# Attention over 128 queries a step, from queries, keys and values that the host lays out, with the softmax sums from a column of ones

## The chip, the cores and the metric

The kernel runs on one NeuronCore of a Trainium2 chip (trn2), as one program. The number that counts is the device time of one execution in microseconds (us). The core has five engines that run beside each other, each in its own instruction order: TensorE (PE in the rows: matrix products and the weight loads, PEld, that go with them), VectorE (DVE), ScalarE (ACT), GpSimd (POOL) and SyncE (SP, which here issues nearly all transfers). 16 DMA engines move data between the chip's memory (HBM) and the on-chip SBUF. Products land in PSUM, which has eight banks of 512 32-bit numbers in each of 128 partitions.

## The reference, cut to what matters

Three layers follow each other: a windowed attention, a mixture of 8 experts in which each token goes to at most one, and a dense layer of two matrices. The change is in the attention and in how the attention is joined to the routing of the experts.

```python
# q, k, v: [2, 8, 768, 64]  (batch, heads, sequence, head size), float32
k_sum = k.reshape(B, H, nb, 32, D).max(axis=3)          # 24 blocks of 32 keys
v_sum = v.reshape(B, H, nb, 32, D).mean(axis=3)
scores_l = scale * q @ k.T     # kept where |query - key| < 16, -1e9 elsewhere
scores_s = scale * q @ k_sum.T + np.log(32)
a = softmax(concat(scores_l, scores_s))                 # sum + 1e-9 below
x = a @ concat(v, v_sum)       # -> [1536 tokens, 512]
# routing: do_compute = x @ w_skip > 0 ; expert = argmax(x @ w_gate) ; gate = its softmax
x[do_compute] += gate * (relu(x @ w1[e]) @ w2[e])
h = x @ w_in ; out = (max(h,0) + alpha * min(h,0)) @ w_out   # w_in, w_out given as float64
```

## The kernel before, in words

`tile_kernel` has four stages. **Attention** works on 64 queries of all 8 heads at a time, in 24 sub-steps (`subs`, 12 for each batch entry). For a sub-step, 96 keys around the queries and the 24 block keys make 120 columns (`NK`). `sub_s` puts the mask into one PSUM bank with a 16-bit product, and adds four products over it, one for each pair of heads: the two heads of a pair stand in the 128 rows of the array, and `qbd` holds their queries block-diagonally, so half of each weight tile is zeros. DVE takes the row maxima, ACT the exponentials with their sums (`accum_out`), POOL divides by the sums (`sub_n`). `sub_t` turns the result by four PE transposes, ACT copies it, and `sub_x` multiplies it with the values, eight products with 64 weight columns each (L327). Two sub-steps fill 128 tokens, which go out to HBM (`xd`) and are turned once more (`tile_xt`); `tile_lt` and `tile_lg` compute their routing logits, in two products with a copy between.

Queries, keys and values arrive as the reference holds them. So keys and queries are copied into another order (`stage`), turned on PE (`first_k`, `prep_k`, `prep_q`), and copied into windows or into `qbd`; the values come as 256-byte pieces (`load_vwin`).

The order of all engines in this stage is the order of the code (`manual_schedule`): a loop over the sub-steps in which the parts of several sub-steps are interleaved, with lists `todo[n]` for what else belongs to sub-step n (loads, preparation, and the 12 weight pieces of 1 MB each that are loaded ahead). `late` and `after` put copies off to a later place. SP issues transfers in that order too; an issue that waits holds back all behind it. The rows of DMA issues wait for the one eight places before.

**Routing** turns logits into lists: `route_a` (best expert), `route_b` (ranks, on PE), `route_l` (places and gates), `route_c` (one-hot rows), `route_d` (the lists, on PE). It runs for four groups of token tiles, the last two after the last sub-step. `route_end` writes the lists (`lidx`), and eight products that nobody reads follow (`warm`, L542). **Experts** gather the rows of `xd` by the lists and work through 8 experts; their weights come through a ring of buffers whose pieces are released as experts finish. **The dense layer** closes the kernel. The last two stages aren't touched by the change.

Of the kernel before, what the change touches and what calls it, by code (L numbers as in the profile page):

```python
# [22 lines left out]

def bf16_parts(x, n):
    out = []
    for _ in range(n):
        b = (np.float32(x).view(np.uint32) + np.uint32(0x8000)) & np.uint32(0xFFFF0000)
        h = float(b.view(np.float32))
        out.append(h)
        x = x - h  # L30
    return out


@with_exitstack
def tile_kernel(ctx: ExitStack, tc: tile.TileContext, q, k, v, w_skip, w_gate, w1, w2, w_in, w_out, alpha, out):
    nc = tc.nc
    B, H, S, D = q.shape
    NP = H // 2
    NS = S // 64
    NB = S // 32  # L40
    NC = S // 256
    NK = 120
    LT = 3
    LX = 4
    NV = 4
    RB = 4
# [28 lines left out]
    qbd = []  # L75
    for i in range(2):
        qbd.append(apool.tile([128, 4, NP, 2, 64], F32, name=f"qbd{i}"))

    def clear(t, eng):
        eng.memset(t[0:64, :, :, 1, :], 0.0)  # L80
        eng.memset(t[64:128, :, :, 0, :], 0.0)

    clear(qbd[0], nc.vector)


    sel = apool.tile([67, 128], BF16, name="sel")
    nc.gpsimd.memset(sel, 1.0)
    nc.gpsimd.memset(sel[0:64, :], 0.0)
    nc.gpsimd.affine_select(
        out=sel[0:64, :].rearrange("p (h x) -> p h x", h=2), in_=sel[0:64, :].rearrange("p (h x) -> p h x", h=2),  # L90
        pattern=[[0, 2], [-1, 64]], compare_op=ALU.not_equal, fill=1.0, base=0, channel_multiplier=1,
    )
    mask = apool.tile([67, 3, NK], BF16, name="mask")
    nc.gpsimd.memset(mask, 0.0)
    logs = bf16_parts(math.log(32.0), 3)
    mlog = mask[64:67, :, 96:NK]
    nc.gpsimd.memset(mlog, logs[0])
    for i in (1, 2):
        nc.gpsimd.affine_select(
            out=mlog, in_=mlog, pattern=[[0, 3], [0, NK - 96]], compare_op=ALU.not_equal, fill=logs[i],  # L100
            base=-i, channel_multiplier=1,
        )
    for a, off in enumerate((0, 16, 32)):
        m = mask[0:64, a, 0:96]
        nc.gpsimd.affine_select(
            out=m, in_=m, pattern=[[-1, 96]], compare_op=ALU.is_gt, fill=-1.0e9,
            base=off + 16, channel_multiplier=1,
        )
        nc.gpsimd.affine_select(
            out=m, in_=m, pattern=[[1, 96]], compare_op=ALU.is_gt, fill=-1.0e9,  # L110
            base=16 - off, channel_multiplier=-1,
        )

    wg = const.tile([128, KC, 32], F32, name="wg")
    nc.gpsimd.memset(wg, 0.0)
    clear(qbd[1], nc.gpsimd)

    avg = apool.tile([128, 16 + NB], F32, tag="lt", bufs=2, name="avg")
    nc.gpsimd.memset(avg, 1.0 / 32.0)
    nc.gpsimd.affine_select(  # L120
        out=avg, in_=avg, pattern=[[-16, 16 + NB]], compare_op=ALU.is_ge, fill=0.0, base=256, channel_multiplier=1)
    nc.gpsimd.affine_select(
        out=avg, in_=avg, pattern=[[16, 16 + NB]], compare_op=ALU.is_ge, fill=0.0, base=15 - 256, channel_multiplier=-1)

    def win(s):
        return (0, 0) if s == 0 else ((2, 32) if s == NS - 1 else (1, 16))

# [56 lines left out]
    def first_k(c):  # L184
# [19 lines left out]
        if c == 1:  # L204
            for g in range(NP):
                for r in range(2):
                    part(kb[g], 64, 0, 1)
# [1096 lines left out]
```

## Time and profile before

| | us |
|---|---|
| median of 3 runs (lowest, highest) | 544.69 (544.65, 547.13) |
| the profiled execution | 544.38 |
| its span, first to last instruction | 542.6 |
| attention, to the end of the last logits product | about 104.3 |
| rest of the attention and the routing, to the lists | 104.3 to 123.3 |
| experts, and the change-over to the dense layer | 127.5 to about 300 |

Busy shares of the whole span are PE 92%, DVE 58%, POOL 36%, ACT 30%, but a stage has its own limit, and the stages follow each other. A row of the timeline merges instructions of one line: its start, its length and the count of records. A float32 product has two records (an 8-product line shows x16), a transpose or a 16-bit product one. As products are pipelined, the cost of a line is read from its start to the start of the next, and not from its length, which has the latency of the last product in it.

### The profile page before, as it was taken

To read this page: it belongs to the slowest core of one execution; us is meant where nothing else is said; L and a number is where in the kernel's file an instruction comes from. 1 tells how busy PE (TensorE), PEld (TensorE's weight loads), DVE (VectorE), ACT (ScalarE), POOL (GpSimd) and SP (SyncE) were. 2 spreads that over 40 slices of the span, in tenths; PEclk is the share of its full clock that TensorE was granted. 3 is DMA by queue.
4 is the path that set the end of the run, shared out by engine and by line. 5 is a ranking of instruction groups with operands and counts; after the bars stand their busy time and mean duration, and the time that the engine had idled before them with its cause. 6 is when DMAs were issued, how large, how long until landed. Compare 5 with 4: busy or idle time off the path is not lost.

```text
span 542.6 us, 8283 instructions
## 1 busy us (share of the span) xinstructions
PE 498.7 (92%) x2999; PEld 372.7 (69%) x2999; DVE 313.4 (58%) x632; ACT 164.9 (30%) x452; POOL 193.9 (36%) x196
## 2 busy tenths in 40 slices
PE   7988999978899999596499899999999999999997
PEld 5577888853454454265277788888888888888885
DVE  4579666476431854289999739893624324243333
ACT  3666677730011110333444442531120101101010
POOL 5285523336220310324853244733453221212121
PEclk9989999998999999898879999999999999999999
DMA  9899979863999583484445402210000000001022
GB/s 240 229 257 247 278 208 277 240 212 109 383 390 396 183 296 118 150 267 143 136 156 170 142 0 79 77 39 1 0 1 0 2 0 2 0 1 59 20 77 77
DMA packets 66820, 76.81 MB, mean 142 GB/s; under 512 B 23358, under 2 KB 46930, under 8 KB 66764
## 3 DMA queue, kind: packets, MB, share of 16 engines
q1 hardware_dynamic: 55916, 59.67, 35.4%
q10 hardware_dynamic: 9408, 14.68, 8.5%
q0 software_dynamic: 1440, 1.76, 1.0%
q8 instruction: 29, 0.48, 0.4%
q14 instruction: 27, 0.22, 0.1%
HBM read 71.00 MB, written 7.91 MB: 145 GB/s over the span
## 4 chain that ended last, share of the span: by engine, by line
PE 49%; DVE 4%; POOL 2%; issue 1%; DMA 1%; ACT 1%; ACTq 0%; POOLq 0%; DVEq 0%
PE o L1242 24%; PE g L1219 24%; POOL wl L1183 1%; DMA raw<-in_moe_w_in_dram 1%; PE ph L945 1%; DVE f L643 1%; DVE f L649 1%; DVE f L648 1%; DVE xl L1081 1%; DVE acc L1252 1%; PE x2p L1204 0%; DVE f L641 0%; POOL glo L1227 0%; ACT raw L644 0%; ACT acc L1250 0%
## 5 line engine op out<-in xcount | busy, mean ns | idle before, releaser
L1227 POOL TENSOR_TENSOR glo<-gs,ghi 128x512 fp32r<-128x512 f32 x48 | 66.7, 1390 | 157.1 <-ACT ghi L1225 157.1
L1222 DVE TENSOR_SCALAR gs<-g,al 128x512 f32<-128x512 f32 x48 | 35.9, 749 | 109.7 <-PE g L1219 109.7
L1225 ACT CAST ghi<-gs 128x512 fp32r<-128x512 f32 x48 | 29.9, 622 | 176.4 <-PE o L1242 150.9
L1242 PE MATMUL o<-woh,ghi 128*128 128x512 f32 x192 | 76.3, 397 | 5.3 <-ACT ghi L1225 5.3
L1242 PE MATMUL o<-woh,glo 128*128 128x512 f32 x192 | 76.4, 398 | 3.0 <-POOL glo L1227 3.0
L1242 PE MATMUL o<-wl,ghi 128*128 128x512 f32 x192 | 76.4, 398 | 0.0
L1219 PE MATMUL g<-xh,wih 128*128 128x512 f32 (+1 forms) x196 | 53.6, 395 | 2.7 <-DVE xl L1081 1.4
L1219 PE MATMUL g<-xl,wih 128*128 128x512 f32 (+1 forms) x196 | 53.0, 390 | 1.1 <-DVE xl L1081 1.1
L1219 PE MATMUL g<-xh,wl 128*128 128x512 f32 (+1 forms) x196 | 51.5, 385 | 0.0
L1242 PEld LDWEIGHTS o<-woh,ghi 128*128 128x128 f32 x192 | 36.4, 190 | 13.7 <-ACT ghi L1225 5.5
L1219 PEld LDWEIGHTS g<-xh,wih 128*128 128x128 f32 x196 | 36.8, 190 | 11.4 <-issue 1.7
L1242 PEld LDWEIGHTS o<-woh,glo 128*128 128x128 f32 x192 | 36.3, 189 | 11.9 <-POOL glo L1227 3.8
L1219 PEld LDWEIGHTS g<-xl,wih 128*128 128x128 f32 x196 | 36.6, 188 | 9.5 <-DVE xl L1081 1.5
L1242 PEld LDWEIGHTS o<-wl,ghi 128*128 128x128 f32 x192 | 36.5, 190 | 8.2
L1219 PEld LDWEIGHTS g<-xh,wl 128*128 128x128 f32 x196 | 36.4, 188 | 7.8
L945 PE MATMUL ph<-w,gTa 128*64 128x512 f32 x128 | 32.9, 626 | 9.4 <-PEq L1148 5.5
L305 POOL TENSOR_TENSOR p<-p,sm 128x480 f32<-128x480 f32 x23 | 24.1, 1049 | 47.2 <-DVE sm L304 21.5
L293 ACT ACTIVATE p<-s,nm 128x120 f32<-128x120 f32 x96 | 33.5, 365 | 22.7 <-DVE sm L303 19.7
L644 ACT ACTIVATE raw<-raw 128x512 f32<-128x512 f32 x32 | 21.7, 684 | 42.6 <-DVE f L643 41.0
L1223 DVE SCALAR_TENSOR_TENSOR gs<-g,gs 128x512 f32<-128x512 f32 x48 | 33.0, 687 | 1.0
L1183 POOL TENSOR_TENSOR wl<-f,wih 128x512 fp32r<-128x512 f32 x16 | 23.3, 1462 | 20.7 <-ACT wih L1182 18.7
L648 DVE SCALAR_TENSOR_TENSOR f<-raw,f 128x512 int32<-128x512 int32 x32 | 30.4, 954 | 0.3
(213 smaller groups left out, 816.4 us busy)
## 6 DMA issues: line engine op xcount, KB each, us to landing
w<-in_moe_w_dram SPq DMA_DIRECT2D x30, 1024.0 KB
raw<-in_moe_w_in_dram ACTq DMA_DIRECT2D x14, 512.0 KB
raw<-in_moe_w_out_dram ACTq DMA_DIRECT2D x14, 512.0 KB
vt<-in_v_dram SPq DMA_DIRECT2D x24, 192.0 KB
rawqst<-in_q_dram SPq DMA_DIRECT2D x6, 512.0 KB
rawkst<-in_k_dram SPq DMA_DIRECT2D x6, 512.0 KB
xd<-x SPq DMA_DIRECT2D x12, 256.0 KB
out_dram<-acc SPq DMA_DIRECT2D x12, 256.0 KB
```

The costliest lines, as they stand in the source:

```text
L293: nc.scalar.activation(p[:, g, :], sp[:, g, :], AF.Exp, bias=nm[:, g:g + 1], scale=1.0, accum_out=sm[:, g:g + 1])
L305: eng.tensor_tensor(out=p, in0=p, in1=sm.to_broadcast([128, NP, NK]), op=ALU.mult)
L644: nc.scalar.activation(raw.bitcast(F32)[:, :, 0], raw.bitcast(F32)[:, :, 1], AF.Abs)
L648: nc.vector.scalar_tensor_tensor(out=f, in0=m1, scalar=-0x40000000, in1=f, op0=ALU.bitwise_and, op1=ALU.bitwise_or)
L945: nc.tensor.matmul(hp[e][64 * h:64 * h + 64, :], gT[g][:, kc, o:o + 64], a[kc // 2][:, kc % 2, 512 * h:512 * h + 512], start=(kc == 0), st ...
L1183: nc.gpsimd.tensor_tensor(out=lo, in0=f, in1=hi.bitcast(F32), op=ALU.subtract)
L1219: nc.tensor.matmul(ph[:, o], a[:, kc, :], x[kc // 2][:, kc % 2, o], start=(i == 0), stop=(i == 3 * KC - 1))
L1222: nc.vector.tensor_scalar(out=g, in0=ph, scalar1=0.0, scalar2=al[:, j:j + 1], op0=ALU.min, op1=ALU.mult)
L1223: nc.vector.scalar_tensor_tensor(out=g, in0=ph, scalar=0.0, in1=g, op0=ALU.max, op1=ALU.add)
L1225: nc.scalar.copy(ghi, g)
L1227: nc.gpsimd.tensor_tensor(out=glo, in0=g, in1=ghi.bitcast(F32), op=ALU.subtract)
L1242: nc.tensor.matmul(po[i], a[:, o], x, start=(jj == 0 and p == 0), stop=(jj == JC - 1 and p == 2))
```

## The change

The host now lays out its inputs (`layouts`), and only the new layouts are passed: `qt` (queries with the head size in the rows, two heads above each other), `kwin` (for each sub-step of 64 queries the 96 keys, turned, and 24 empty columns), `vwin` (for two sub-steps the 96 value rows, with a 1 behind each head's 64 values), `vtok` and `vblk` (values for the block sums), `wgs` and `als`. The transposes, copies and rearrangements of queries and keys go. `block_k` takes the block maxima from the loaded windows and copies them into the empty columns.

A step has 128 queries, and there are 12. `sub_s` issues four mask products and 16 logits products, each with 64 rows and 64 weight columns: head of the pair r chooses the rows and the PSUM bank, half of the queries c chooses the columns. The exponentials have no `accum_out`: the sum comes out of the value product as its 65th column (block rows hold 32 there, and block sums of values in place of means), and `sub_n` divides the product, on DVE, instead of the probabilities, on POOL. The routing logits are one product over 9 columns for each 128 of the 512 features, in `tile_lg`. `late` and `after`, the weave of the last routing groups and `warm` go; PSUM has three banks for logits, and one (`ps_m`) for all of transposed tokens, routing logits, ranks and lists, where three stood.

```diff
-    ps_s = att.enter_context(tc.tile_pool(name="ps_s", bufs=2, space=PSUM))
+    ps_s = att.enter_context(tc.tile_pool(name="ps_s", bufs=3, space=PSUM))
-    ps_m = att.enter_context(tc.tile_pool(name="ps_m", bufs=3, space=PSUM))
+    ps_m = att.enter_context(tc.tile_pool(name="ps_m", bufs=1, space=PSUM))
...
+    def load_k(b, g):
+        kw[b, g] = (kpool, apool)[b].tile([128, NS, NK], F32, tag=f"kw{g}", name=f"kw{b}_{g}")
+        nc.sync.dma_start(kw[b, g], kwin[b, g])
+    def block_k(b, g, spread):
+        m = apool.tile([128, NB], F32, tag="km", bufs=2, name=f"km{b}_{g}")
+        nc.vector.tensor_reduce(
+            out=m.rearrange("p (s n) -> p s n", s=NS),
+            in_=kw[b, g][:, :, 16:80].rearrange("p s (n i) -> p s n i", n=2), axis=AX.X, op=ALU.max)
+        spread(out=kw[b, g][:, :, NWK:NK], in_=m[:, None, :].to_broadcast([128, NS, NB]))
...
-        nc.tensor.matmul(sp, sel, mask[:, win(s)[0], None, :].to_broadcast([67, NP, NK]), start=True, stop=False)
-        for g in range(NP):
-            nc.tensor.matmul(
-                sp[:, g, :], d[:, s % 4, g].rearrange("p h x -> p (h x)"), kw[b, g][:, s, :], start=False, stop=(g == NP - 1))
+        for c in range(2):
+            for r in range(2):
+                s = 2 * t + c
+                w = 0 if s == 0 else (2 if s == NS - 1 else 1)
+                nc.tensor.matmul(
+                    sp[r][64 * c:64 * c + 64], sel[64 * r:64 * r + 64, :],
+                    mask[64 * r:64 * r + 64, w, None, :].to_broadcast([64, NP, NK]), start=True, stop=False)
+        for g in range(NP):
+            for c in range(2):
+                for r in range(2):
+                    o = 128 * (t % 2) + 64 * c
+                    nc.tensor.matmul(
+                        sp[r][64 * c:64 * c + 64, g, :], qs[64 * r:64 * r + 64, g, o:o + 64],
+                        kw[b, g][64 * r:64 * r + 64, 2 * t + c, :], start=False, stop=(g == NP - 1))
...
-            nc.scalar.activation(p[:, g, :], sp[:, g, :], AF.Exp, bias=nm[:, g:g + 1], scale=1.0, accum_out=sm[:, g:g + 1])
+            nc.scalar.activation(
+                p[:, g, :], st["s", n][r][:, g, :], AF.Exp, bias=st["nm", n][:, r, g:g + 1], scale=1.0)
...
-        eng.tensor_tensor(out=p, in0=p, in1=sm.to_broadcast([128, NP, NK]), op=ALU.mult)
+    def sub_x(n):
+        st["x", n] = xp = ps_x.tile([128, 2, 512], F32, tag="x", name=f"xp{n}")
+        for h in range(H):
+            for c in range(2):
+                nc.tensor.matmul(
+                    xp[64 * c:64 * c + 64, h // 4, DV * (h % 4):DV * (h % 4) + DV],
+                    ts[h % 2][:, h // 2, 64 * c:64 * c + 64], vt[b][:, 2 * (t % 2) + c, h, :], start=True, stop=True)
+    def sub_n(n):
+        x = st.pop(("x", n))[:, :, 0:4 * DV].rearrange("p k (h e) -> p k h e", h=4)
+        nc.vector.tensor_scalar(out=sm, in0=x[:, :, :, D:DV], scalar1=1e-9, scalar2=None, op0=ALU.add)
+        nc.vector.reciprocal(out=sm, in_=sm)
+        nc.vector.tensor_tensor(
+            out=t.rearrange("p (k h d) -> p k h d", k=2, h=4), in0=x[:, :, :, 0:D],
+            in1=sm.to_broadcast([128, 2, 4, D]), op=ALU.mult)
+        nc.sync.dma_start(xd[128 * n:128 * n + 128, :], t)
...
+        for c in range(KC):
+            nc.tensor.matmul(ps, xT[:, c, :], wg[:, c, :], start=(c == 0), stop=(c == KC - 1))
...
+    load_q(0, 0)
+    for g in range(NP):
+        load_k(0, g)
+    for c in range(NCH):
+        load_vtok(c)
...
+    for n in range(TT):
+        sub_s(n)
+        if n >= 3:
+            tile_xt(n - 3)
+        sub_m(n)
+        sub_e(n, 0)
+        if n >= 1:
+            sub_t(n - 1, 0, V)
+            sub_t(n - 1, 1, A)
+        sub_e(n, 1)
+        if n >= 2:
+            sub_x(n - 2)
+            sub_n(n - 2)
+        if n >= 3:
+            tile_lg(n - 3)
+        for f in todo[n]:
+            f()
...
+    n = TT - 1
+    tile_xt(n - 2)
+    sub_t(n, 0, V)
+    sub_t(n, 1, A)
+    sub_x(n - 1)
+    sub_n(n - 1)
+    tile_lg(n - 2)
+    for f in todo[TT]:
+        f()
+    sub_x(n)
+    tile_xt(n - 1)
+    route_a(*G[2])
+    sub_n(n)
+    tile_lg(n - 1)
+    route_b(*G[2])
+    route_l(*G[2], [])
+    tile_xt(n)
+    tile_lg(n)
+    for t in range(*G[2]):
+        route_c(t)
+    route_d([4, 5, 6, 7])
+    route_a(*G[3])
+    route_b(*G[3])
+    route_l(*G[3], range(*G[3]))
+    route_d(list(range(8, TT)))
+    route_end()
-    warm(WARM[2])
```
```

On PE, a sub-step of the kernel before in its steady part stands so (the names: `s` logits, `pt` transposed probabilities, `xp` the value product, `qps` transposed queries, `lt` routing products):

```order
L284 LDWEIGHTS sel
L284 MATMUL s_3_1099<-mask,sel 128x480
L286 MATMUL s_3_1099<-kw_0_520,qbd_87 128x120
L286 MATMUL s_3_1099<-kw_1_585,qbd_87 128x120
L286 MATMUL s_3_1099<-kw_2_646,qbd_87 128x120
L286 MATMUL s_3_1099<-kw_3_766,qbd_87 128x120
L311 MATMUL pt_0_1116<-ident,p_0_949 120x128 x4
L327 MATMUL xp_10_1076<-vt_131,ts_11_1095 64x64 x8
L268 MATMUL qps_2_0_1130<-ident,qst_2_1085 128x128 x4
L432 MATMUL lt_1137<-xT_1097,wg 32x128 x4
```

In the changed kernel the end of the logits of one step of 128 queries, and what follows on PE, stand so (four mask products `L171` and 14 more rows of `L178` stand ahead of it, and six more of `L210` and the four products of `tile_lg` behind it):

```order
L178 MATMUL s_0_1139<-kw_3_502,q_2_877 64x120
L178 MATMUL s_1_1140<-kw_3_502,q_2_877 64x120
L281 MATMUL xtp_1161<-ident,x_1114 128x128 x4
L199 MATMUL pt_0_1176<-ident,p_0_1070 120x128 x4
L199 MATMUL pt_1_1183<-ident,p_1_1089 120x128 x4
L210 MATMUL xp_1195<-vt_111,ts_0_1080 64x65 x2
L210 MATMUL xp_1195<-vt_111,ts_1_1087 64x65 x2
```

A logits product has become four of a quarter the tile, the two value products of 64 queries have become one set that alternates between the halves of the array, and `qps` and `lt` are gone from the row.

On DVE, the last routing before the lists is woven in the kernel before: the one-hot rows (`ohb`) stand between steps of `route_a` and ahead of the copies of logits (`lg`):

```order
L502 TENSOR_TENSOR loc<-r_s_1788,r_s_1706 128x2
L488 CAST val<-r_es_1780 128x2
L514 TENSOR_SCALAR ohb_1794<-rows,loc 128x512
L443 COPY lg<-lg_1771 128x9
L443 COPY lg<-lg_1799 128x9
L452 TENSOR_REDUCE r_mx_1802<-lg 128x2
L454 TENSOR_SCALAR r_act_1804<-lg 128x2
L456 TENSOR_TENSOR r_ex_1806<-lg,r_mx_1802 128x16
L459 TENSOR_TENSOR r_oh_1809<-lg,r_mx_1802 128x16
L461 TENSOR_SCALAR r_s_1811<-r_act_1804 128x2
L462 TENSOR_TENSOR r_oh_1809<-r_oh_1809,wt 128x16
L514 TENSOR_SCALAR ohb_1794<-rows,loc 128x512
```

In the changed kernel, at the same place, the copy of the last logits comes first, and the one-hot rows and the sum of lists (`acc`) stand ahead of the last `route_a`:

```order
L351 TENSOR_TENSOR loc<-r_s_1485,r_s_1446 128x2
L337 CAST val<-r_es_1477 128x2
L290 COPY lg<-lg_1498 128x9
L358 TENSOR_SCALAR ohb_1504<-rows,loc 128x512
L358 TENSOR_SCALAR ohb_1506<-rows,loc 128x512
L375 TENSOR_TENSOR acc<-acc,lps_1508 128x20
L301 TENSOR_REDUCE r_mx_1527<-lg 128x2
L303 TENSOR_SCALAR r_act_1529<-lg 128x2
L305 TENSOR_TENSOR r_ex_1531<-lg,r_mx_1527 128x16
```

So DVE has the same instructions there, but waits for PE (`lg`, `acc`) before work that is ready.

## Rows read from the trace of the kernel before

**Rows 1.** Windows: length, busy us of engines, granted clock, DMA share, GB/s.

```profile
2.50:15.00 12.50, 10.35 (x67) 8.48 (x65) 6.25 (x9) 3.58 (x9) 5.35 (x14) 1.00 1.18 290
23.05:104.30 81.25, 77.12 (x800) 67.85 (x800) 55.09 (x154) 57.35 (x233) 39.31 (x58) 0.98 0.94 250
104.30:123.30 19.00, 14.98 (x228) 11.86 (x227) 14.87 (x83) 7.71 (x24) 5.32 (x5) 0.91 0.72 243
123.30:127.50 4.20, 3.40 (x9) 0.91 (x7) 3.47 (x18) 0.00 (x0) 2.96 (x3) 0.57 0.27 95
127.50:240.00 112.50, 101.17 (x616) 50.85 (x616) 52.77 (x105) 16.71 (x30) 27.13 (x24) 0.98 0.72 259
140.00:177.00 37.00, 34.41 (x198) 17.26 (x195) 10.60 (x22) 3.05 (x6) 3.50 (x4) 1.00 1.04 388
```

**Rows 2.** Timeline of PE, from 15 us: start, length, instruction, records.

```profile
17.79 5.33 PE L231 MATMUL vps<-rawvst,avg 128*24 128x512 f32 x12
24.59 0.37 PE L284 MATMUL s<-mask,sel 67*128 67x480 bf16 x1
```

**Rows 3.** Timeline of PE, three sub-steps from 86 us.

```profile
86.13 0.38 PE L284 MATMUL s<-mask,sel 67*128 67x480 bf16 x1
86.34 1.05 PE L286 MATMUL s<-kw,qbd 128*128 128x120 f32 x8
87.23 0.60 PE L311 MATMUL pt<-ident,p 128*120 128x128 f32 x4
87.76 1.15 PE L327 MATMUL xp<-vt,ts 120*64 120x64 f32 x16
88.84 0.39 PE L442 MATMUL lg<-fold,lts 128*128 128x9 f32 x2
89.08 0.63 PE L420 MATMUL xtp<-ident,x 128*128 128x128 f32 x4
...
92.37 0.43 PE L432 MATMUL lt<-xT,wg 128*32 128x128 f32 x8
92.73 0.19 PE L519 MATMUL lps<-none,ones 128*128 128x20 bf16 x1
...
96.40 0.36 PE L284 MATMUL s<-mask,sel 67*128 67x480 bf16 x1
```

**Rows 4.** Timeline of PE, experts.

```profile
130.48 0.46 PE L996 MATMUL lb<-val,ohb 128*128 128x5 bf16 x12
130.87 1.94 PE L945 MATMUL ph<-w,gTa 128*64 128x512 f32 x8
...
163.28 5.42 PE L1015 MATMUL phb<-w,xt_more 128*128 128x512 f32 x12 [0.51 <-ACT xt_more L894]
226.57 3.26 PE L945 MATMUL ph<-w,gTa 128*64 128x512 f32 x8 [5.46 <-PEq L1148]
```

**Rows 5.** Timeline of DVE, end of attention and routing.

```profile
104.29 0.66 DVE L289 TENSOR_REDUCE nm<-s 128x4 f32<-128x480 f32 x1 [2.40 <-PE s L286]
...
107.73 0.18 DVE L452 TENSOR_REDUCE r_mx<-lg 128x4 f32<-128x32 f32 x1
...
109.05 0.18 DVE L493 TENSOR_REDUCE r_es<-r_ex 128x4 f32<-128x32 f32 x1
...
111.19 0.19 DVE L497 TENSOR_TENSOR r_sl<-rk,ob 128x32 f32<-128x32 f32 x1 [1.55 <-PE rk L478]
...
113.86 1.31 DVE L514 TENSOR_SCALAR ohb<-rows,loc 128x512 bf16<-128x512 f32 x2
...
123.19 0.17 DVE L546 SCALAR_TENSOR_TENSOR lidx<-acc 128x4 int32<-128x4 f32 x1
```

**Rows 6.** Instructions grouped by line and shape, to 140 us.

```profile
L293 ACT ACTIVATE p<-s,nm 128x120 f32<-128x120 f32 x96 | 33.5, 365 | 22.7 <-DVE sm L303 19.7 <-DVE nm L289 2.9
L289 DVE TENSOR_REDUCE nm<-s 128x4 f32<-128x480 f32 x24 | 15.7, 656 | 25.2 <-PE s L286 25.1
```

**Rows 7.** Transfers to 128 us.

```profile
DMA packets 43181, 30.58 MB, mean 239 GB/s; under 512 B 21170, under 2 KB 36550, under 8 KB 43164
```

More of the change, by code (lines that the diff above doesn't have):

```diff
@@ L72, in tile_kernel @@
+    V, A, P = nc.vector.tensor_copy, nc.scalar.copy, nc.gpsimd.tensor_copy
+    xs, st, kw, qc, vt, vbk = {}, {}, {}, {}, [], {}
     ident = const.tile([128, 128], F32, name="ident")
     make_identity(nc, ident)
[L75 to L86, printed above, removed]
@@ L98, in tile_kernel @@
[L98 to L112, printed above, removed]
@@ new lines, in load_vtok, with sum_pe @@
+    def load_vtok(c):
+        t = kpool.tile([128, 2, DM], F32, tag="raw", bufs=4, name=f"vtok{c}")
+        nc.sync.dma_start(t, vtok[:, c])
+        st["vtok", c] = t
+    def sum_pe():
+        ps = ps_t.tile([128, 512], F32, tag="t", name="vps")
+        for c in range(NCH):
+            raw = st.pop(("vtok", c))
+            for r in range(2):
+                nc.tensor.matmul(
+                    ps[96:NK, :], ones32[:, 16 - 8 * c:16 - 8 * c + NB], raw[:, r, :],
+                    start=(c == 0 and r == 0), stop=(c == NCH - 1 and r == 1))
+        A(vt[0][96:NK, 0, :, 0:D], ps[96:NK, :].rearrange("n (h d) -> n h d", h=H))
+        for j in range(1, 4):
+            nc.sync.dma_start(vt[0][96:NK, j], vt[0][96:NK, 0])
@@ L661, in fill @@
             next(steps)
[L664 to L669 removed]
+    HOT = 22
     def hot(n):
[L672 to L673 removed]
+        t = ps_x.tile([128, 2, 512], F32, tag="x", name="hot")
         for i in range(n):
[L675 to L676 removed]
+            nc.tensor.matmul(
+                t[:, i % 2, 0:256], ident.bitcast(BF16)[:, 0:128], ident.bitcast(BF16)[:, 0:256], start=True, stop=True)
@@ L678, in tile_kernel @@
     ms = ExitStack()
     ms.enter_context(tc.manual_schedule())
-    load(q, 0, 0, "qst")
-    for c in range(NC):
-        load(k, 0, c, "kst")
-    hot(HOT[0])
-    stage(0, 0, "qst", 1, V)
-    stage(0, 0, "kst", 3, V)
-    first_k(0)
-    prep_q(0, 0, 0, A)
-    prep_q(0, 0, 1)
-    for c in range(NC):
-        load(v, 0, c, "vst")
-    load(q, 0, 1, "qst")
-    route_loads()
-    flush(after)
-    flush(late)
-    stage(0, 1, "kst", 3, V)
-    hot(HOT[1])
-    first_k(1)
-    hot(HOT[2])
@@ L718, in tile_kernel @@
-    NN = len(subs)
-    todo = {n: [] for n in range(-8, NN + 24)}
+    load_q(0, 0)
+    for g in range(NP):
+        load_k(0, g)
+    for c in range(NCH):
+        load_vtok(c)
+    load_vwin(0)
+    load_vwin(1)
+    load_q(0, 1)
+    nc.sync.dma_start(wg, wgs)
+    nc.sync.dma_start(al, als)
+    hot(HOT)
+    scale_q(0, 0, nc.scalar, slice(0, 128))
+    for g in range(NP):
+        block_k(0, g, A)
+    scale_q(0, 0, nc.gpsimd, slice(128, QW))
+    scale_q(0, 1, nc.gpsimd)
+    todo = {n: [] for n in range(-1, TT + 4)}
@@ L737, in tile_kernel @@
[L737 to L750 removed]
+    plan(0, sum_pe)
+    plan(1, load_q, 0, 2)
```

527 lines of the change are left out of this document (138 added, 389 removed).

## The prediction

> **What bounds the kernel now.** I read the windows by stage first, because busy shares of the whole span mix stages. In the attention loop (23 to 104 us, [rows 1]) PE is busy 77.1 of 81.25 us, DVE 55, ACT 57 and POOL 39, and the DMA share is 0.94 at only 250 GB/s. So PE sets the pace, with the transfers close behind. In the stretch of the last routing (104 to 123 us, [rows 1]) no engine fills its time: that is a chain of small steps between PE, DVE and ACT. In the experts (127.5 to 240 us, [rows 1]) PE is busy 101 of 112.5 us. That stage and the dense layer have the same work after the change, so what counts is how much earlier or later the lists are written (`lidx` at 123.19 us, [rows 5]), and whether the experts then start as well as before.
>
> The timeline of PE gives the price of a sub-step. Three sub-steps go from 86.13 to 96.40 us [rows 3], 3.42 us each or 6.85 us for 128 queries. With the preparation of the second batch in it, the whole loop runs from the third sub-step at 24.59 us [rows 2] to the last logits, whose reader on DVE starts at 104.29 us [rows 5]: 79.7 us for 22 sub-steps, or 7.25 us for 128 queries.
>
> **Start.** Before the first product, the changed kernel loads the queries (0.52 MB) and four window tiles (128x1440 numbers, 0.74 MB each): 3.47 MB. At 290 GB/s, the rate of the first transfers before (2.5 to 15 us, [rows 1]), that takes 12.0 us, at the 388 GB/s that the weight pieces reach (140 to 177 us, [rows 1]) 8.9 us; from 2.5 us on, 11.4 to 14.5 us. The maximum over 768 numbers is taken at the price of the one over 480, 656 ns [rows 6], so 1.05 us; with a copy of 288 numbers and the last products at about 1 us together, the first logits stand at 13.5 to 16.5 us; I take 15. The block sums of the values (5.33 us of PE, [rows 2]) stay and follow there, so the second step starts at about 20.3 us. It has the queries of the third and fourth sub-step, which started at 24.59: some 4.3 us won. That is less than the removed transposes and copies suggest, since both kernels wait for the block sums.
>
> **A step of 128 queries on PE.** Prices from start to start [rows 3]: logits 0.89 us for 8 records, 0.111 each; transposes 0.53 for four; value product 1.08 for 16, 0.0675 each; logits of the routing 0.24 for two, 0.12 each; the `lt` products 0.36 for 8, 0.045 each; a mask product 0.21. The prices go with the weight columns (128: 0.111 and 0.12; 64: 0.0675; 32: 0.045) although the streamed columns differ (120, 9, 64, 128).
>
> - Logits: 16 products, 32 records, each on a quarter of the array. The trace before has no product on half the rows. It shows that the two column halves work side by side: 512 streamed columns cost 1.94/8 = 0.24 us a record where the halves alternate (L945) and 5.42/12 = 0.45 us at full width (L1015) [rows 4]. Bounds: at the best, the shortest spacing in these rows, 0.39/12 = 0.032 us (L996 to the next line, [rows 4]), 1.03 us; at the worst no overlap, 32 x 0.111 = 3.55 us. The nearest rows are 0.045 (column groups beside each other) and 0.0675 (same weight width, one group); I take 0.053, so 1.70 us. The four mask products cost 0.21 (all beside each other) to 0.84; I take 0.35.
> - Transposes of the probabilities: 8, as before, 1.06. Transposes of the tokens: 4, 0.53.
> - Value product: 32 records with 64 weight columns, now alternating between the halves: 0.045 to 0.0675, taken 0.058, 1.85 us (before 2.16).
> - Routing logits: 8 records of 128 weight columns at 0.12, 0.96 us, where `lt` and its second product cost 0.36 + 0.24.
>
> Sum 6.45 us against 7.25. So the rearranged products win little; the win is that the transposes of queries and keys go. The Trainium skill (TensorE: Matmul & The Clock Gate, Part 3, "The mechanism") says that a weight load overlaps a running product only where the row groups differ. The trace does not agree: the 8 logits records of the kernel before use all rows and still cost 0.111 us each [rows 3], less than a load of that width (0.12 us with 9 streamed columns) and its product one after the other. So I count no extra gain from the alternating rows.
>
> The other engines stay below 6.45 us a step. ACT has 8 exponentials at no more than 365 ns [rows 6] and two copies, some 4.1 us; the reads of the sums go. DVE has two maxima (1.31), a copy, the division and the copy of logits, some 3.2 us. Logits of step n+1 need the first exponentials of step n (three banks for two each): logits 2.05, maximum 0.66, four exponentials 1.46, so 4.3 us a round. That holds only in the first step. Dividing on DVE in place of POOL is thus covered by PE's other work, and if it weren't, the price is the division, about 1.05 us a step.
>
> Sum: second step from 20.3; this step 4.3; the next without token transposes and routing logits 4.95; eight full steps 51.6; the first group's routing 3.0 (its `route_a` on DVE, 109.05 - 107.73 = 1.32 us [rows 5], now has PE waiting for it in the order, and list products of four tiles). So the last logits start at 84.2 and end at 86.2 us, 18.1 us earlier than 104.3.
>
> **After the last logits.** Before, 104.29 to 123.19 is 18.9 us [rows 5]. In the changed order, counted from the end of the last logits: token transposes, probabilities' transposes, value product of step 9 and its division, 4.7; routing logits copied and `route_a`, 6.2; `route_l` (0.55 + 1.1 after the ranks, [rows 5]) 8.0; two one-hot rows (1.31 us for two, [rows 5], at the least 0.95) 9.0; the last probabilities copied, value product 10 and its division 11.95; only then, since there is one buffer for the product, value product 11 at 14.0, and its division, behind `route_a` of the third group, 15.4; ranks and places of that group, which share one bank with the logits of token tile 10, 18.2; transposes, copy, logits and copy for tile 11, 19.7; two one-hot rows 20.7 and the sum of lists; only then the last `route_a` 22.1, ranks and `route_l` 23.8, one-hot rows 24.8, lists and `lidx` 25.6. That is 6.7 us more than before. The bounds: 18.9 (all waits hidden) and 29 (products at half the price's speed in a stretch with idle PE). So `lidx` is at 111.8 us, 11.4 earlier.
>
> **Clock.** The granted clock was 0.57 at 123.3 to 127.5 us [rows 1], with eight unread products in it, and these are gone. Eight products that follow a 5.46 us gap of PE took 3.26 us instead of 1.94 [rows 4]: 1.3 us. I take 1.5 for the first products of the experts, 0 to 3 as bounds.
>
> **Transfers.** 30.58 MB moved until 128 us, and 21170 of 43181 packets were under 512 bytes [rows 7]. The windows hold 5.9 MB where the keys had 3.1, so it is some 33.3 MB now, in pieces of 2 KB and more, needed by 112 us: 300 GB/s, below the 388 of the weight pieces. I count nothing.
>
> Forecast: 544.38 (the profiled execution; the median of the runs is 0.31 above) - 11.4 + 1.5 = 534.5 us.
>
> **Rivals.**
>
> 1. The quarters of the array load and work beside each other to the full. Logits then cost 1.03 + 0.21, value products 32 x 0.045 = 1.44, a step 5.26 us: 9.5 us less over eight steps, some 4 in the first two, the last and the end: 521 us. For it: the halves do so (L945). Against: the price by weight columns. The Trainium skill has this as a rule (TensorEngine Tiling (Array Packing), "Key Properties": different tiles can load weights and multiply in parallel); no row here has two row tiles.
> 2. Each record pays the full price of 64 weight columns, 0.0675: logits 2.16 + 0.4, value products 2.16, a step 7.27 us. Then 0.82 x 8 and some 2.7 at both ends are lost: 544 us, no change; the shorter start is spent on the longer end.
> 3. Slower: the logits don't overlap at all, 0.111 a record and 0.84 for the masks, 4.39 us a step; 2.65 x 8 and 8 in the other steps more than forecast: 564 us. It decides from about 0.08 us a record on, where the 9.9 us won are spent over 11 steps. Against it: L945.
> 4. The transfers stay at 250 GB/s: 33.3 MB take until 136 us, and the experts start up to 8 us later than before: 553 us. Against: packet sizes.
>
> **Chances.** Forecast 0.45 (its own range 528 to 541), first rival 0.25, second 0.13, third 0.10, fourth 0.07. Under 0.5% (2.7 us), a measurement of this kernel can't tell a change. Faster by more: 0.45 + 0.25 + 0.05 of the second = 0.75; within: 0.05 of the second and 0.02 of the fourth = 0.07; slower 0.18. The range 519 to 549 leaves out the third rival, half of the fourth and the edge of the first.
>
> **What would show it.** The second step's mask products start at 19 to 22 us. In the middle of the loop, mask products of consecutive steps are 6 to 7 us apart, with PE never idle for long; from `L178`'s first start to the next line it is 1.7 us (1.0: first rival; 2.2: second; 3.5: third). From the last logits to `lidx` it is 24 to 28 us. Wrong would be: PE waiting in the loop for ACT, DVE or windows, or a step that is set by anything but PE; or experts and dense layer that take over 3 us more or less than 419 us from `lidx` to the end.

## The result: slower by 1%, and the profile after

The changed kernel takes 550.46 us (median of 4 runs, 549.11 to 551.84), the kernel before 544.67 (4 runs). The ratio is 1.010 (95% interval 1.006 to 1.015): slower, where 534.5 us was forecast. The profiled execution took 549.11 us (span 547.3).

The products became cheaper than forecast. One step in the middle of the changed loop, on the timeline of PE (start, length, instruction, records):

```profile
56.20 0.40 PE L171 MATMUL s<-mask,sel 64*64 64x480 bf16 x4
56.43 0.99 PE L178 MATMUL s<-kw,q 64*64 64x120 f32 x32
57.35 0.66 PE L281 MATMUL xtp<-ident,x 128*128 128x128 f32 x4
57.84 1.04 PE L199 MATMUL pt<-ident,p 128*120 128x128 f32 x8
58.81 1.15 PE L210 MATMUL xp<-vt,ts 120*64 120x65 f32 x32
59.89 1.06 PE L289 MATMUL lg<-wg,xT 128*128 128x9 f32 x8
60.88 0.40 PE L171 MATMUL s<-mask,sel 64*64 64x480 bf16 x4
```

From mask to mask it is 4.68 us for 128 queries; two sub-steps before took 6.85 [rows 3]. The 32 logits records take 0.92 us to the next line (0.029 each), the 32 value records 1.08 (0.034).

But such a step is rare. The windows of the changed kernel (the columns are those of [rows 1]) are the first transfers, the loop from the second step's masks to the last logits, the rest up to the lists, and three stretches of the loop:

```profile
2.50:15.00 12.50, 7.99 (x58) 4.05 (x56) 5.03 (x6) 2.88 (x8) 3.82 (x8) 0.81 1.02 409
20.54:100.56 80.02, 56.90 (x885) 49.88 (x885) 38.99 (x99) 31.12 (x100) 27.99 (x36) 0.78 0.92 289
100.56:127.14 26.58, 17.67 (x227) 15.45 (x227) 17.13 (x88) 6.01 (x17) 0.17 (x1) 0.76 0.69 223
20.00:25.00 5.00, 4.42 (x84) 3.04 (x83) 1.83 (x4) 3.06 (x10) 4.75 (x10) 1.00 0.14 32
34.00:45.00 11.00, 0.44 (x5) 0.20 (x2) 3.00 (x5) 0.19 (x1) 7.32 (x15) 0.66 1.03 365
45.00:50.00 5.00, 4.79 (x60) 4.52 (x64) 3.60 (x8) 2.61 (x9) 0.00 (x0) 0.50 1.01 345
```

In the loop PE is busy for 57 of 80 us, at a granted clock of 0.78, where before it was 77 of 81 at 0.98 [rows 1]. From 34 to 45 us it does next to nothing while the DMA share is 1.03. The view of waits, behind the first loads, says for what (engine, line, releaser: us in total, times, longest):

```profile
PE xp L210 <- DMA vt<-in_vwin_dram: 20.4, 4, 10.8
DVE km L114 <- DMA kw<-in_kwin_dram: 9.8, 2, 8.5
```

So PE waits for windows of values, and VectorE for keys of the second batch entry. What comes behind such a wait, on PE's timeline, and the queue of SP at three places (start, length, instruction):

```profile
45.20 2.00 PE L210 MATMUL xp<-vt,ts 120*64 120x65 f32 x32 [10.76 <-DMA vt<-in_vwin_dram]
...
49.34 1.81 PE L178 MATMUL s<-kw,q 64*64 64x120 f32 x32
...
94.47 2.00 PE L210 MATMUL xp<-vt,ts 120*64 120x65 f32 x32 [5.04 <-DMA vt<-in_vwin_dram]
...
132.72 3.68 PE L705 MATMUL ph<-w,gTa 128*64 128x512 f32 x8 [0.46 <-ACT gTa L654]
```

```profile
11.51 0.33 SPq L514 DMA_DIRECT2D al<-in_als_dram  x1
21.31 2.81 SPq L134 DMA_DIRECT2D vt<-vt  x3
...
39.61 0.33 SPq L152 DMA_DIRECT2D vbd<-vbk  x1
39.99 0.91 SPq L110 DMA_DIRECT2D kw<-in_kwin_dram  x2
...
80.81 0.52 SPq L430 DMA_DIRECT2D w<-in_w_dram  x1
81.39 1.13 SPq L433 DMA_DIRECT2D w<-in_w_dram  x2
82.63 0.94 SPq L161 DMA_DIRECT2D vt<-in_vwin_dram  x1
```

Behind the wait the clock is 0.50 (window 45 to 50 us), the lower of its two levels (1.2 of 2.4 GHz), and the rows of the same logits and values are 1.81 and 2.00 us long (0.99 and 1.15 in the step above). The window that is late at 94.47 was issued at 82.63, behind three weight pieces of 1 MB. Between 11.51 and 21.31 us SP issues nothing: the copies of the block sums (L134) stand next in its queue, and they wait 9.4 us for ScalarE. So from 20 to 25 us, where the loop begins, the transfer engines move only 32 GB/s, at a share of 0.14. The write of the second batch's sums (39.61) waited for GpSimd in the same way, with two key loads behind it. The last two rows on VectorE that answer to [rows 5], and the transfers to 128 us, which answer to [rows 7]:

```profile
100.56 1.22 DVE L186 TENSOR_REDUCE nm<-s 128x4 f32<-128x480 f32 x2 [2.07 <-PE s L178]
...
127.14 0.17 DVE L379 SCALAR_TENSOR_TENSOR lidx<-acc 128x4 int32<-128x4 f32 x1
```

```profile
DMA packets 13562, 35.42 MB, mean 277 GB/s; under 512 B 2340, under 2 KB 3364, under 8 KB 13548
```

The last maximum starts 3.7 us earlier than before (100.56, 104.29), the lists stand 3.95 us later, and the first products of the experts take 3.68 us where such a set took 1.94 before [rows 4]. From the lists to the end of the span it is 420.2 us, as before (419.4).

### The profile page after: what moved, and what is told of

Read it like the earlier page. It is cut to its first block, busy times and chain, and to the rows that moved or that the text cites. A ratio compares the mean times of both kernels' runs of the same rounds, so it can differ in the third digit from the quotient of the medians.

```text
span 547.3 us, 8063 instructions
## 1 busy us (share of the span) xinstructions
PE 475.5 (87%) x3068; PEld 351.7 (64%) x3068; DVE 293.3 (54%) x570; ACT 132.4 (24%) x297; POOL 173.8 (32%) x161
## 3 DMA queue, kind: packets, MB, share of 16 engines
q1 hardware_dynamic: 25036, 62.50, 33.5%
## 4 chain that ended last, share of the span: by engine, by line
PE 48%; DVE 4%; POOL 2%; issue 1%; DMA 1%; ACT 1%; ACTq 0%; POOLq 0%; DVEq 0%
PE o L1002 24%; PE g L979 23%; POOL wl L943 1%; DMA raw<-in_w_out_dram 1%; PE ph L705 1%; DVE f L475 1%; DVE f L481 1%; DVE f L480 1%; DVE xl L841 1%; DVE acc L1012 1%; PE x2p L964 0%; DVE f L473 0%; POOL glo L987 0%; ACT raw L476 0%; ACT acc L1010 0%
## 5 line engine op out<-in xcount | busy, mean ns | idle before, releaser
L979 PEld LDWEIGHTS g<-xh,wih 128*128 128x128 f32 x196 | 36.2, 187 | 10.4 <-ACT xh L840 1.2
L705 PE MATMUL ph<-w,gTa 128*64 128x512 f32 x128 | 34.4, 661 | 8.0 <-PEq L908 5.4
L210 PE MATMUL xp<-vt,ts 120*64 120x65 f32 x384 | 17.4, 257 | 22.6 <-DMA vt<-in_vwin_dram 20.4
L210 PEld LDWEIGHTS xp<-vt,ts 120*64 120x64 f32 x384 | 15.6, 168 | 25.1 <-issue 18.3
L191 ACT ACTIVATE p<-s,nm 128x120 f32<-128x120 f32 x96 | 27.2, 386 | 14.6 <-DVE nm L186 14.6
```

The source lines that it names most:

```text
L191: nc.scalar.activation(p[:, g, :], st["s", n][r][:, g, :], AF.Exp, bias=st["nm", n][:, r, g:g + 1], scale=1.0)
L210: nc.tensor.matmul(xp[64 * c:64 * c + 64, h // 4, DV * (h % 4):DV * (h % 4) + DV], ts[h % 2][:, h // 2, 64 * c:64 * c + 64], vt[b][:, 2 * ...
L705: nc.tensor.matmul(hp[e][64 * h:64 * h + 64, :], gT[g][:, kc, o:o + 64], a[kc // 2][:, kc % 2, 512 * h:512 * h + 512], start=(kc == 0), st ...
L979: nc.tensor.matmul(ph[:, o], a[:, kc, :], x[kc // 2][:, kc % 2, o], start=(i == 0), stop=(i == 3 * KC - 1))
```

## Experiments

Theory A: the loop waits for transfers because of their order in SP's queue. Rival B: the bytes as such are too many for the loop. Rival C: the price of the products and of the longer tail. Beside them the clock behind each wait. Times below are medians of the runs; ratios are to the kernel before.

**Weights out of the loop (e2_late).**

```diff
-        plan(PLAN[i], load_weights, 1)      # twelve pieces, steps 1 to 11
...
     sub_n(n)                               # last token write
+    load_weights(NR[0] + NR[1])
```

> The changed kernel with its twelve 1 MB weight pieces taken out of the loop and issued behind the last write of a token tile; nothing else moves. Theory A (order): the first wait (10.8 us at 34 to 45 us, with one weight piece and the keys ahead of the window) loses about 3 to 4 us, the later ones (4.1, 0.4, 5.0 and 2.3 us, where pieces stand ahead of the window) go: lidx at 114 to 119 us, total 537 to 545, the experts perhaps waiting a little for weights that are issued only at about 100 us. Rival B (bytes): 12.6 MB fewer in the loop, every wait goes, lidx at 105 to 112. Rival C (products and tail): lidx within 3 us of 127.

534.27 us, 0.980 (0.974 to 0.986). The loop, and then VectorE's list and the experts' start:

```profile
21.00:82.92 61.92, 50.98 (x886) 44.73 (x886) 38.81 (x100) 31.04 (x100) 27.01 (x35) 0.89 0.75 236
```

```profile
106.75 0.17 DVE L379 SCALAR_TENSOR_TENSOR lidx<-acc 128x4 int32<-128x4 f32 x1
...
114.07 1.11 PE L651 MATMUL gpa<-ident,xg 128*128 128x128 f32 x4 [6.83 <-DMA xg<-xd,lidx]
```

The lists stand 20.4 us earlier, beyond what A expected: B's range, although a first wait of 6.0 us is left. Rival C is out: the same products and the same tail. In the total some 4.2 us of that come back, most of it because the gather now shares the engines with the weights (7.3 us from the lists to the first transposes; 4.0 in the changed kernel).

**The same in the kernel before (e7_before_late).** The same edit on the kernel before: its twelve pieces behind the last values of the loop.

> The kernel before with its twelve weight pieces taken out of the loop and issued behind the last token write, as in e2_late. If the kernel before is bound by TensorE in its loop (77.1 of 81.3 us busy), lidx stays within 2 us of 123.2 and the first expert starts up to 3 us later behind it since the gather shares the engines with the weights: total 544 to 549 us. If the transfers held the kernel before as they hold the changed one, it gets faster by more than 4 us.

```profile
23.05:104.89 81.84, 76.89 (x799) 67.62 (x798) 54.83 (x153) 57.16 (x233) 38.89 (x58) 0.98 0.59 142
```

```profile
123.78 0.17 DVE L546 SCALAR_TENSOR_TENSOR lidx<-acc 128x4 int32<-128x4 f32 x1
...
153.90 1.11 PE L891 MATMUL gpa<-ident,xg 128*128 128x128 f32 x4 [26.61 <-DMA xg<-xd,lidx]
```

With 142 GB/s in place of 250 [rows 1], the loop takes as long as before: there the weights were hidden behind PE. The total, 570.42 us (1.045, 1.039 to 1.052), tells nothing on that: the pieces came to stand ahead of the last two token writes in SP's queue (130.72 us), and the gather waited 26.6 us for these. A total of 544 to 549 was expected, so the edit was put in the wrong place.

**Windows first (e14_window_first), block sums late (e15_late_sums).** One part of the order each.

```diff
# e14
             sub_x(n - 2)
+            load_vwin(n)
             sub_n(n - 2)                   # token write; loads of the step follow
# e15
-    nc.sync.dma_start(vbd[...], t[:, 0, :])     # in sum_v, steps 3 and 5
+    plan(5, write_sums)                         # both writes
```

> The changed kernel with one thing moved: a step's window of values is issued right behind the product that frees its slot, ahead of the token write, the weight pieces and the other loads of that step. If what stands ahead of the windows is what costs, the waits of L210 (10.8, 4.1, 0.4, 5.0 and 2.3 us) fall to about 6 us in all, most of that the first, and lidx is at 117 to 122 us, total 540 to 546. If the engines are busy with the same bytes anyway, the windows come sooner but the keys, queries and weights as much later: lidx within 3 us of 127.

> The changed kernel with one thing moved: the block sums of the second batch are written to DRAM at step 5, both together, instead of at steps 3 and 5, so the queue is not held for GpSimd at 32 to 39.6 us with keys, queries and a window behind the write. If that hold costs, the wait for keys (8.5 us of DVE) and the wait at tile 3 go, lidx 3 to 6 us earlier, total 544 to 548. If it stood behind the wait for the second window (10.8 us) anyway, lidx is within 2 us of 127 and the total within 549 to 552.

550.54 us (1.009, 1.004 to 1.013) and 551.8 (1.009, 1.006 to 1.012): no gain. `lidx` is at 127.64 and 129.94 us. Waits of e14, and its timelines of PE and VectorE around the first:

```profile
PE xp L210 <- DMA vt<-in_vwin_dram: 16.1, 5, 6.0
DVE km L114 <- DMA kw<-in_kwin_dram: 12.8, 3, 10.4
```

```profile
41.24 2.00 PE L210 MATMUL xp<-vt,ts 120*64 120x65 f32 x32 [5.96 <-DMA vt<-in_vwin_dram]
...
49.00 2.20 PE L178 MATMUL s<-kw,q 64*64 64x120 f32 x32
```

```profile
43.35 0.95 DVE L114 TENSOR_REDUCE km<-kw 128x24 f32<-128x768 f32 x1 [10.41 <-DMA kw<-in_kwin_dram]
```

The window came 4.0 us earlier, the keys 2.8 us later (43.35; 40.55 in the changed kernel), and the next logits start at 49.00 us as in the changed kernel (49.34). In e15 the windows waited 21.3 us in all. Theory A, in the form that one misplaced transfer holds the loop, falls.

**The whole order (e1_order), with all weights in the loop; with the weights out (e4_both).**

```diff
+    load_k(1, 0); load_k(1, 1)             # at the start
+    plan(0, load_vblk, i)                  # before: step 1
+            load_vwin(n)                   # behind sub_x, as e14
+    plan(6, write_sums)
+    plan(7, put_v)
```

> Same transfers and bytes as the changed kernel, in another order of SyncE's queue: half of the second batch's keys are issued at the start and the block values at step 0, ahead of the copies that wait for the block sums; a step's window of values is issued right behind the product that frees its slot, ahead of the token write and the weight pieces; the second batch's block sums are written to DRAM at step 6 instead of holding the queue at step 3 and 5. Theory A (the loop waits for windows and keys that stand late in an in-order queue): the waits of L210 for windows, 20.4 us in four places, fall under 8 us, lidx is done at 112 to 119 us (127.1 in the changed kernel), total 534 to 542 us. Rival B (the transfers are slow as such: 35 MB wanted in 128 us, whatever the order): the waits move but stay above 14 us in sum, lidx at 123 us or later, total 546 to 552. Rival C (the price of the products and of the longer tail): the waits go and lidx stays above 122 all the same.

> Both edits together: the other order of the queue, and the weight pieces behind the last token write. Under A and B alike the loop then waits for nothing: eleven steps of about 4.7 to 5 us from 20.5 us, last logits done at 75 to 80 us with the first group's routing, tail of 22 to 25 us at the better clock, lidx at 99 to 106 us. The total follows by as much (523 to 530) unless the experts wait for the weights: 12.6 MB issued at about 85 us land by about 120 at 350 GB/s, so a few us may be lost there. Rival C: lidx above 118.

e1_order: 543.88 us, 0.994 (0.991 to 0.998), `lidx` at 121.05, between A and B. The copies of the block sums, now behind 3 MB of other loads, made a new wait:

```profile
32.84 2.00 PE L216 MATMUL xp<-vt,ts 120*64 120x65 f32 x30 [7.11 <-DMA vt<-vt]
```

e4_both: 534.73 us, 0.979 (0.973 to 0.985), `lidx` at 107.68; that is above the 99 to 106 expected: the same wait cost 6.5 us, and the tail took 26.5.

**Order mended, weights in the loop (e5_spread); half of them out (e8_mixed).**

```diff
# e5: the order of e1; copies of the sums by ScalarE and GpSimd; pieces behind the window
+    PLAN = (3, 4, 5, 6, 7, 8, 9, 9, 10, 10, 11, 11)
# e8: third buffer for queries; six pieces in the loop, three behind the last
#     token write, three on ScalarE's queue behind the gathered tokens
+    PLAN = (4, 5, 6, 8, 9, 10)
+    turn_base(0)
+    load_weights(3, nc.scalar)
```

> The changed kernel with the queue's order of e1_order and three mends of what waited there: the block sums of the first batch are copied into the four value windows by ScalarE and GpSimd instead of three DMAs that stood behind 3 MB of other loads; the second batch's sums are written and read back one step earlier (steps 5 and 6); the weight pieces go out at steps 3, 4, 5, 6, 7, 8, 9, 9, 10, 10, 11, 11, behind the window of their step. All 12.6 MB of weights stay in the loop. If it is the order that costs, L210 waits under 3 us in all, lidx is done at 100 to 107 us, the first expert's product starts about 5.6 us later as in the changed kernel (no weights ahead of the gather), total 525 to 533 us. If the bytes cost as such, the loop still waits 8 us or more: lidx at 108 or later, total 535 or more.

> e5_spread with what still waited there taken away: a third buffer for the queries, so that the third query load goes out at the start, ahead of the second batch's keys; six weight pieces in the loop (steps 4, 5, 6, 8, 9, 10) instead of twelve, three behind the last token write, three on ScalarE's queue behind the first expert's gathered tokens. If the loop is bound by the bytes that compete in it, it now waits under 3 us in all: last logits at 75 to 79 us, lidx at 98 to 103, first expert's product 6 us behind, total 523 to 529 us. If order alone were the cause, it would do no better than e5_spread with its wait for the queries gone (lidx 106 to 109, total 531 to 534).

e5_spread: 536.91 us, 0.987 (0.979 to 0.994), `lidx` at 112.86. That is B's side of what was expected, since it is above 108; but all twelve pieces are still issued by the last step, and the lists stand 14.3 us earlier than in the changed kernel, so the order of the queue as a whole counts too. e8_mixed: 521.56 us, 0.955 (0.950 to 0.960). The loop of each, then VectorE in e8:

```profile
20.50:81.79 61.29, 51.91 (x885) 44.90 (x878) 38.79 (x99) 31.48 (x100) 28.62 (x35) 0.89 0.98 302
```

```profile
20.50:75.09 54.59, 49.54 (x885) 43.34 (x878) 40.65 (x99) 31.52 (x100) 28.70 (x35) 0.94 0.98 315
```

```profile
75.09 1.22 DVE L190 TENSOR_REDUCE nm<-s 128x4 f32<-128x480 f32 x2 [1.02 <-PE s L182]
...
99.06 0.17 DVE L383 SCALAR_TENSOR_TENSOR lidx<-acc 128x4 int32<-128x4 f32 x1
```

Both loops keep the transfer engines at a share of 0.98. In e5 PE still waited 6.2 us for queries, in the loop, and 5.3 for windows, behind it; in e8 0.6 us for a window. e8 differs from e5 by the bytes, by the third query buffer and by earlier query loads, so these are not told apart; but e5 with its 6.2 us given back would still be at 106.7, an estimate that takes the whole wait off `lidx`.

**Fillers in the waits (e3_hot).**

```diff
         if n >= 2:
+            hot({4: 85, 7: 30, 10: 38}.get(n, 0))
             sub_x(n - 2)
```

> The changed kernel with filler products on TensorE (128x256 bf16 on a constant, into the bank of the values product) where it waits for windows: 85, 30, 38 and 16 of them ahead of the products of tiles 2, 5, 8 and 11, some 9.1, 3.2, 4.1 and 1.7 us of work inside waits of 10.8, 4.1, 5.0 and 2.3 us. What it tells: the share of the clock. If the half clock behind each wait costs (one step took 7.26 us there instead of 4.68), lidx comes 3 to 7 us earlier, at 120 to 124, and the total is 543 to 547. If the transfers set the pace anyway, the steps behind a wait get shorter and the next wait longer by as much: lidx within 1.5 us of 127, total 549 to 552.

```profile
40.00:50.00 10.00, 8.44 (x124) 7.38 (x123) 6.12 (x12) 2.61 (x9) 3.18 (x4) 1.00 1.02 363
```

```profile
127.65 0.17 DVE L379 SCALAR_TENSOR_TENSOR lidx<-acc 128x4 int32<-128x4 f32 x1
```

The clock is 1.00 there instead of 0.50, and `lidx` is where it was; 551.18 us, 1.012 (1.005 to 1.019). In this loop, which waits for transfers, the clock behind the waits cost nothing that can be seen; I had counted it as a second loss.

**Records of one quarter behind each other (e11_grouped)**, from e9_tail below.

```diff
-        for g in range(NP):
-            for c in range(2):
-                for r in range(2):
+        for c in range(2):
+            for r in range(2):
+                for g in range(NP):
```

The value products likewise, all heads of one column half first.

> e9_tail with the same logits and values products in another order: the 32 logits records of a step no longer go round the four 64x64 quarters of TensorE but eight by eight in one quarter, and the values records sixteen by sixteen in one column half. It tells what the low price per record rests on (32 logits records 0.92 us from start to the next form, 32 values records 1.08, in e9_tail). If neighbours in different quarters overlap and those in one quarter don't, the logits take 1.6 us or more (0.05 us for 120 columns at full clock each) and up to 3.6 (32 records at the 0.111 us of a 128-column record), the values 1.2 to 3.6: a step is 1 to 5 us longer, the last maximum comes 10 us or more later than in e9_tail, total 528 us or more. If the order of the records doesn't matter, both stay at about 1 us and the total within 1.5 per cent of e9_tail.

538.97 us, 0.992 (0.989 to 0.994), where e9_tail has 518.28. A step of e11_grouped on PE, and the one of e9_tail that answers to it:

```profile
38.63 0.40 PE L175 MATMUL s<-mask,sel 64*64 64x480 bf16 x4
38.86 2.38 PE L182 MATMUL s<-kw,q 64*64 64x120 f32 x32
41.17 0.66 PE L292 MATMUL xtp<-ident,x 128*128 128x128 f32 x4
...
42.63 1.90 PE L214 MATMUL xp<-vt,ts 120*64 120x65 f32 x32
44.46 1.06 PE L300 MATMUL lg<-wg,xT 128*128 128x9 f32 x8
45.45 0.40 PE L175 MATMUL s<-mask,sel 64*64 64x480 bf16 x4
```

```profile
32.62 0.40 PE L175 MATMUL s<-mask,sel 64*64 64x480 bf16 x4
32.85 0.99 PE L182 MATMUL s<-kw,q 64*64 64x120 f32 x32
33.77 0.66 PE L292 MATMUL xtp<-ident,x 128*128 128x128 f32 x4
```

Logits take 2.31 us instead of 0.92 (0.072 a record, 0.029), values 1.83 instead of 1.08 (0.057, 0.034), a step 6.82 instead of 4.68. Two sub-steps of the kernel before took 6.85, so the whole win of a step on PE hangs on the order of its records. In the logits a neighbour may differ in row half, column half and PSUM bank; which of these counts there is not told apart. That different quarters work beside each other is the rule of the Trainium skill (TensorEngine Tiling (Array Packing), "Key Properties") that different tiles load and multiply in parallel, and these rows agree with it.

**The tail (e9_tail, e12_seven, e13_tailfill) and its clock (e6_warm, e10_tailwarm).** e9: from the last step on, the small products use the logits' three banks. e12: one weight piece more in the loop. e13, e6, e10: fillers.

```diff
# e9
+        if tail[0]:
+            return ps_s.tile(shape, F32, tag="s", name=name)
+        return ps_m.tile(shape, F32, tag="m", name=name)
...
# e10
     route_counts()
+    warm(30)
```

> e8_mixed with the tail's small products (token transposes, expert logits, ranks, lists) in the three banks of the logits, which are free by then, instead of the one bank that they share in turn. If the one bank sets the tail's pace, the stretch from the last maximum to lidx falls by 2 to 4 us from e8_mixed's (about 23 to 24 us expected there); if VectorE's chain does, by less than 1 us.

> e9_tail with one weight piece moved from behind the gather into step 11 of the loop. In e9_tail TensorE waits for weights in the third expert (3.1 us and more at 124 to 132 us), so the earlier experts gave back what the attention won. If a piece more in time mends that without a wait in the loop, total 514 to 518 us; if the pieces that are issued after the gather are the late ones all the same, or the loop waits for its last window instead, within 2 us of e9_tail.

> e9_tail with 6, 6, 7 and 7 filler products (128x256 bf16, 0.11 us each at full clock, in the bank that the routing leaves free there) in four waits of the tail. The stretch from the last maximum to lidx was 21.1 us in e9_tail (clock 0.82 there) and 25.5 and 25.3 with the same instructions in e10_tailwarm and e12_seven (0.66 and 0.62). If the clock makes that difference and the fillers hold it up, the stretch takes 19.5 to 22 us at a clock of 0.85 or more. If the fillers stand in the way or the clock falls all the same (it fell in these runs before the first of them), it takes 24 us or more.

> e5_spread with filler products on TensorE in the tail's waits and behind the count product: 7, 6, 7, 6, 7, 7 and 34 of them, 0.11 us each at full clock, in the logits' banks that are free by then. If the half clock costs here (the tail's products and the first expert's product, 3.68 us for eight instead of 1.94, are on the path), lidx comes 1 to 3 us earlier than in e5_spread and the total is 3 to 5 us lower. If the tail is bound by VectorE's chain alone, or the fillers stand in the way, lidx stays within 1 us and the total within 1.5 us.

> e9_tail with thirty filler products (128x256 bf16) behind the count product, while TensorE waits for the first gather. If the half clock of the first expert's products costs, the second expert's first product starts 2 to 3 us earlier behind lidx than in e9_tail and the total is lower by as much; if not, both stay within 1 us.

e9_tail: 518.28 us, 0.948 (0.942 to 0.953), the lowest median, though its runs (514.61 to 522.04) overlap with those of e8_mixed, e10, e12 and e13; e12_seven 520.88, 0.958 (0.954 to 0.962), outside both its forecasts; e13_tailfill 522.21, 0.957 (0.952 to 0.962); e10_tailwarm 521.67, 0.954 (0.948 to 0.960); e6_warm, on e5_spread, 538.67 against 536.91, with the lists at 116.38 against 112.86. From the last maximum to `lidx`: e8 24.0 us, e9 21.1, and with the same tail code e10 25.5 and e12 25.3, e13 24.4. So the banks are not shown to help. The clock in these stretches was 0.77, 0.82, 0.66, 0.62 and 0.85, and PE stood still before the last value product for 1.0 us in e10 (a window) and 1.3 in e13; which of these makes the 4 us stays open, and e13's fillers, at 0.85, bought nothing. What the clock costs behind the lists is shown by e9 and then e10, the products of the first two experts on PE:

```profile
100.23 3.68 PE L720 MATMUL ph<-w,gTa 128*64 128x512 f32 x8 [0.46 <-ACT gTa L669]
...
104.24 1.94 PE L720 MATMUL ph<-w,gTa 128*64 128x512 f32 x8
```

```profile
105.87 1.94 PE L727 MATMUL ph<-w,gTa 128*64 128x512 f32 x8 [0.46 <-ACT gTa L676]
108.13 1.94 PE L727 MATMUL ph<-w,gTa 128*64 128x512 f32 x8
```

Counted from `lidx` (94.61 and 100.11), the second expert's products start after 9.6 and 8.0 us: 1.6 us for thirty fillers, where 2 to 3 were expected. The totals don't show it: in both runs PE stands still for 3 us before a later product (128.78 and 130.90 us), and e10's lists were later.

## Why the prediction was wrong, step by step

- **Start**: the second step's masks were forecast at 20.3 us, they start at 20.54. Right, but partly by luck: the first logits were done at 13.66 us (forecast 15), and the block sums took 6.9 us of PE (forecast 5.33), some of it at a clock of 0.51 to 0.80; the two errors cancel.
- **A step on PE**: forecast 6.45 us, measured 4.68 where nothing waits. Logits 0.92 (forecast 1.70), masks 0.23 (0.35), values 1.08 (1.85), the rest as forecast. These two terms were sized too large, which by itself would have made the kernel faster than forecast. It is the first rival's mechanism, at a price below even its own (5.26). The prediction weighed a rule of the Trainium skill (TensorE: Matmul & The Clock Gate, Part 3, "The mechanism": a weight load overlaps only where row groups differ) and put it aside. These runs fit neither: logits records in alternating quarters are cheap (0.029), so counting no gain was wrong; and so are the value records, which share their rows and alternate only the column half (0.034 against 0.057 in e11_grouped), so a difference in rows is not the only thing that helps. The second rival's price, 0.0675, is close to what a logits record costs when one quarter gets eight in a row (0.072).
- **Transfers**: this step failed. It read "needed by 112 us: 300 GB/s, below the 388 of the weight pieces. I count nothing". So the wait for windows stood at nothing in the sum, although "PE waiting in the loop for ACT, DVE or windows" is named there as a sign of being wrong; it was 20.4 us. An average to 112 us says nothing of the loop. The changed kernel's loop moved 23.1 MB (80.02 us at 289 GB/s). At the 302 to 315 GB/s of the loops of e5_spread and e8_mixed that is an estimated 73 to 77 us, and the forecast loop (20.3 to 86.2 us) has 66. The 388 of [rows 1] belongs to a stretch that moves little but weight pieces. The kernel before had 81 us and PE to hide behind; a faster PE took the cover off. The rest is the order: at the start of the loop, while the block sums are made, next to nothing is moved. Both parts are shown. With the twelve pieces out and the old order the lists stand 20.4 us earlier (e2_late), with all pieces in and a mended order 14.3 (e5_spread), with half of the pieces out and a mended order 28.1 (e8_mixed). In e5_spread the last maximum is at 81.79 us, but the tail then takes 31.1 us and holds the late windows. How the loss divides between bytes and order stays open.
- **Last logits**: forecast to end at 86.2 us; their maximum starts at 100.56. With half the weights out and the order mended it is 75.1, earlier than forecast, since a step is cheaper.
- **Tail**: forecast 25.6 us, measured 26.6; 24.0 in e8_mixed. Near, but the forecast counted neither the clock (0.76) nor 2.25 us in which PE stands still before the last value product (112.96 us). The profile puts these down to `ob` on VectorE, which that product doesn't read; its window was issued only at 106.31 us, so a wait for the window is likely, but not shown.
- **Clock** in the experts: forecast 1.5 us, measured 1.7 (3.68 for 1.94). Right for these products; from the lists to the end it is only 0.8 longer than before, so part of it is given back later.
- **Experts and dense layer**: 419 forecast, 420.2 measured. Right.

The sum: 14.4 us more in the loop, 1.0 more in the tail, 0.7 less behind the lists. The fourth rival had the right resource and, by luck, nearly the total (553), but not the place: the loop's rate was 289 GB/s and not 250, and the experts did not wait for weights; the loop waited for windows and keys. e8_mixed measures the first rival's 521 us, partly by chance: its step is cheaper (4.68 against 5.26), and its transfers still run at a share of 0.98. The third rival's 564 us doesn't follow from its prices: with the other terms as forecast they make a step 2.34 us dearer, not 2.65, so some 561.

## What to carry to other kernels

A prefetch that hides behind a bound engine is free only as long as that engine is slow: when a loop is made shorter, count the bytes inside the new loop, at the rate that its own mix reaches, before counting the gain. Moving one transfer forward in a saturated queue only moved the wait to the next one (e14). What helped here was to take bytes out of the loop (e2), and to arrange the whole queue so that no issue that waits stands ahead of loads that could run (e5). Issue small products so that neighbours fall in different quarters of the array: here the same logits records cost 2.5 times as much when they were grouped, the value records 1.7 times.

## What the runs showed of the hardware

The order of records alone changes a logits record from 0.029 to 0.072 us, and a value record, where only the column half alternates, from 0.034 to 0.057. At a DMA share of 0.98 the loops' mix moved 302 to 315 GB/s, the first loads 409 (at 1.02). And with fillers in PE's waits (clock 1.00 from 40 to 50 us in place of 0.50), nothing was won: the lists stood at 127.65 us against 127.14.
